# Attention blocks of the first tile: transposes, values and placing one round later, normalization last in its round

## Chip, core and metric

The kernel runs on one core of a Trainium2 chip. The time is device microseconds of one execution; the median of several runs is compared. A core has TensorE (PE, with its weight loads as PEld), VectorE (DVE), ScalarE (ACT), GpSimd (POOL) and SyncE (SP), which here only issues DMAs. Each engine takes its instructions in a fixed order and waits on semaphores of the others.

## What is computed

A chunked attention over 4 batches of 8 heads, 768 positions of 64 features, then two dense layers on the 3072 rows of 512 features:

```python
for c in range(nc):                      # chunks of 32 queries, context of 16 left and 8 right
    k_full = concatenate([mem_k, k_ctx]); v_full = concatenate([mem_v, v_ctx])   # 8 memory rows
    scores = scale * q_c @ k_full.T
    a = exp(scores - max(scores)); a = a / (sum(a) + 1e-9)
    out[c] = a @ v_full
x = out.transpose(0, 2, 1, 3).reshape(3072, 512)
h = x @ w_in;  x = (max(h, 0) + log1p(exp(-abs(h)))) @ w_out          # d_ff 2048
y = ((x @ w_a) * (x @ w_b)) @ w_o2                                    # d_ff 1536
```

q, k, v and the first weights come in as 64-bit floats.

## The kernel before

The 3072 rows are eight tiles of 384. For each tile the first layer runs over 16 slots `f`: `emit_h` (L465) makes `ph` with 12 matmuls, ACT and DVE form the softplus `g` in `emit_soft` (L471 to L475, L452, L455), and `emit_x1` (L488) accumulates. The second layer (L520, L540) follows for all eight tiles. Each operand is split in a high and a low part, so three matmuls stand for one product.

Weights arrive as 64-bit words in `raw`. `convert_a` (L102 on ACT, L104 and L105 on DVE) puts them together as 32-bit `tmp`, and `convert_b` (L112 on ACT, L113 on DVE) splits `tmp` into the parts of `w`. The buffers of `raw`, `w`, `work`, `qk` and `afb` are all of one pool of 33.

The attention of the first tile stands ahead of everything. It is cut in six blocks of 64 queries (`Block`), each with these steps:
- `turn`: PE transposes k and q (L278), ACT copies k (L281), DVE copies q (L283).
- `scores`: PE (L290), then DVE's masked row maxima, four of them (L325), then ACT's four exponentials with their sums (L329).
- `normal`: DVE, L333, L334 and L336.
- `flip`: PE transposes the normalized weights (L301), ACT copies them out (L302).
- `values`: PE, L309.
- `place`: ACT's cast (L315) and DVE's difference (L316) write the block's columns of the tile `x` that `emit_h` reads.

`ROUND` says in which order a round runs the steps and for which block: an entry (d, step) in round i is the step of block i - d. One `convert_a` goes behind `turn`, from round 1 on, and one `convert_b` behind `flip`, from round 2 on. What the rounds have not converted by then comes behind them, up to ten first halves and nine second halves. All five engines follow this order as it is written, up to the end of the first tile; the loads of the blocks and weights are issued by SP ahead of it, at most eight outstanding. The first tile's loop then mixes the 16 slots with conversions and with the attention steps of the second tile.

Of the kernel before, what the change touches and what calls it, by code (L numbers as in the profile page):

```python
# [25 lines left out]
               (1, "values"), (2, "place"))  # L26
EARLY, EARLY_AT, EARLY_BY = 3, 14.5, 8.25

ROUND = ((2, "normal"), (4, "place"), (0, "turn"), (2, "flip"), (1, "scores"), (3, "values"))
EARLY_RAW = (0, 1, 2, 3, 5, 7)  # L30
W_BY = (3, 2, 2, 2)
AHEAD = 6
# [7 lines left out]
def attn_moe_moe2(ctx: ExitStack, tc: tile.TileContext, q, k, v, mem_k, mem_v,  # L40
# [15 lines left out]
    BPT = TT // QB  # L56
# [492 lines left out]
    def order():  # L549
# [20 lines left out]
        def convert_1(half):  # L570
            if n_cv[half] < len(uses):
                (convert_a, convert_b)[half](*uses[n_cv[half]])
                n_cv[half] += 1

        for i in range(BPT + 4):
            for d, step in ROUND:
                if 0 <= i - d < BPT:
                    getattr(blocks[i - d], step)()
                if i >= CV_ROUND and step == "turn":
                    convert_1(0)  # L580
                if i > CV_ROUND and step == "flip":
                    convert_1(1)
# [79 lines left out]
        for fn, p in jobs:  # L662
            fn(*p)

    order()


# [28 lines left out]
```

## Time and profile before

| what | value |
|---|---|
| median of three runs | 1312.18 us (1309.62 to 1312.55) |
| profiled execution | 1311.32 us, span 1309.5 us |
| PE busy, share of the span | 1237.2 us, 94% |
| DVE, ACT, POOL busy | 473.4, 534.7, 247.6 us |
| chain that ended last, by engine | PE 84%, DVE 5%, SP's queue 3%, ACT 3%, DMA 3% |

The rows further down are from one profiled execution. Times are microseconds from the start of the span; 1.8 us of the profiled time lie outside the span. A busy time is an engine's own time in instructions; what an engine waits for is told in brackets behind the row. The ends of PE's rows are modelled.

### The profile page before, as it was taken

The page shows a single profiled execution, that of the slowest core. Times are in us where ns is not written, and L with a number is a line of the kernel's source. Part 1 is how long each engine was busy: PE and PEld are TensorE (multiplying, and loading weights), DVE is VectorE, ACT ScalarE, POOL GpSimd, SP SyncE. Part 2 cuts the span into 40 slices and gives each one's busy share as a digit, 9 for nine tenths or more (in the row PEclk, how much of TensorE's full clock was granted, in tenths as well). Part 3 has the DMA queues.
Part 4 walks back from the last instruction along what each step waited for, and adds up shares of the span by engine and source line. Part 5 has one row for each costly group of instructions (what it writes and reads, how often), then busy time and mean ns, then how long its engine had stood idle before and what let it go on. Part 6 is the DMA issues. An engine that isn't in the chain of part 4 may idle for free.

```text
span 1309.5 us, 20027 instructions
## 1 busy us (share of the span) xinstructions
PE 1237.2 (94%) x7872; PEld 1170.1 (89%) x7872; DVE 473.4 (36%) x1283; ACT 534.7 (41%) x1328; POOL 247.6 (19%) x233
## 2 busy tenths in 40 slices
PE   5768799999999999999798999999999999999998
PEld 4667699999999999999798999999999999999997
DVE  4767544544444454544678410111101011011100
ACT  4767556555556556554685211111111111111111
POOL 1000023223222322323001011211212121121111
PEclk9879899999999999999899999999999999999999
DMA  8872412213041312211775000010101001000000
GB/s 175 205 246 60 90 37 46 54 35 72 12 73 37 60 48 36 62 23 41 241 227 175 1 26 25 1 49 1 49 1 41 9 10 40 1 25 1 25 1 25
DMA packets 170169, 77.99 MB, mean 60 GB/s; under 512 B 137691, under 2 KB 162395, under 8 KB 170075
## 3 DMA queue, kind: packets, MB, share of 16 engines
q1 hardware_dynamic: 169563, 76.64, 22.1%
q8 instruction: 62, 1.02, 0.3%
q14 instruction: 32, 0.26, 0.1%
q0 software_dynamic: 512, 0.07, 0.0%
HBM read 64.09 MB, written 12.58 MB: 59 GB/s over the span
## 4 chain that ended last, share of the span: by engine, by line
PE 84%; DVE 5%; SPq 3%; ACT 3%; DMA 3%; issue 1%; DVEq 0%; ACTq 0%
PE pab L520 31%; PE ph L465 18%; PE px L488 17%; PE py L540 15%; DMA raw<-in_moe_w_out_dram 2%; PE sc L372 1%; PE pxa L415 1%; SPq L267 1%; DVE w L113 1%; DVE tmp L105 1%; ACT e L472 1%; SPq L264 1%; ACT e L471 1%; ACT e L473 1%; DVE g L475 0%
## 5 line engine op out<-in xcount | busy, mean ns | idle before, releaser
L520 PE MATMUL pab<-x,w 128*128 128x384 f32 x2304 | 418.8, 336 | 4.1 <-issue 4.1
L520 PEld LDWEIGHTS pab<-x,w 128*128 128x128 f32 x2304 | 405.9, 188 | 12.6 <-issue 4.4
L465 PE MATMUL ph<-x,w 128*128 128x384 f32 x1536 | 298.3, 342 | 13.5 <-ACT x L422 8.2
L465 PEld LDWEIGHTS ph<-x,w 128*128 128x128 f32 x1536 | 272.9, 192 | 20.1 <-ACT x L422 9.4
L529 DVE TENSOR_TENSOR c<-pab,a 128x384 f32<-128x384 f32 x96 | 53.6, 558 | 493.5 <-PE pab L520 493.5
L475 DVE SCALAR_TENSOR_TENSOR g<-ph,e 128x384 f32<-128x384 f32 x128 | 71.2, 557 | 257.0 <-ACT e L473 253.3
L527 ACT COPY a<-pab 128x384 f32<-128x384 f32 x96 | 46.1, 480 | 260.4 <-PE pab L520 260.4
L471 ACT ACTIVATE e<-ph 128x384 f32<-128x384 f32 x128 | 62.3, 486 | 132.2 <-PE ph L465 119.5
L390 DVE STREAM_TRANSPOSE af<-sm 32x256 f32<-32x256 f32 x180 | 78.2, 435 | 2.5
L473 ACT ACTIVATE e<-e 128x384 f32<-128x384 f32 x128 | 67.3, 526 | 3.8
L472 ACT ACTIVATE e<-e 128x384 f32<-128x384 f32 x128 | 67.3, 526 | 3.8
L329 ACT ACTIVATE sm<-sm,st 128x96 f32<-128x96 f32 x168 | 60.5, 362 | 4.7 <-DVE st L325 4.7
L505 POOL TENSOR_TENSOR x<-xr,x 128x1536 fp32r<-128x1536 f32 x8 | 28.4, 3554 | 153.5 <-DVE x L504 148.7
L105 DVE SCALAR_TENSOR_TENSOR tmp<-raw,tmp 128x512 uint32<-128x512 uint32 x68 | 50.2, 739 | 14.4 <-ACT raw L102 11.0
L113 DVE TENSOR_TENSOR w<-tmp,w 128x512 fp32r<-128x512 f32 x68 | 46.9, 689 | 16.9 <-ACT w L112 16.8
L102 ACT ACTIVATE raw<-raw 128x512 f32<-128x512 f32 x68 | 45.4, 673 | 15.4 <-DMA raw<-in_moe_w_in_dram 7.1
L112 ACT CAST w<-tmp 128x512 fp32r<-128x512 f32 x68 | 41.6, 613 | 17.2 <-DVE tmp L105 17.1
L195 POOL DMA_DIRECT2D mem_n<-in_mem_k_dram x16 | 8.9, 560 | 155.8 <-DVE mem_t L353 155.8
L336 POOL TENSOR_TENSOR sm<-sm,st 128x768 f32<-128x768 f32 x18 | 26.5, 1472 | 60.1 <-DVE st L334 46.9
L104 DVE TENSOR_SCALAR tmp<-raw 128x512 uint32<-128x512 uint32 x68 | 31.9, 469 | 5.0 <-DMA raw<-in_moe_w_in_dram 4.6
L325 DVE CUSTOM_DVE_ANT_0 sm<-sc,mask 128x96 f32<-128x96 f32 x168 | 31.4, 253 | 3.8 <-PE sc L372 3.8
L329 ACT ACTIVATION_READ_ACCUMULATOR sm<-sm,st 128x1 f32 x168 | 31.4, 187 | 0.0
(251 smaller groups left out, 1851.7 us busy)
## 6 DMA issues: line engine op xcount, KB each, us to landing
raw<-in_moe_w_out_dram SPq DMA_DIRECT2D x28, 512.0 KB
raw<-in_moe_w_in_dram SPq DMA_DIRECT2D x16, 512.0 KB
vn<-in_v_dram SPq DMA_DIRECT2D x35, 176.0 KB
raw<-in_moe_w_a_dram SPq DMA_DIRECT2D x12, 512.0 KB
x_scratch<-xo SPq DMA_DIRECT2D x32, 192.0 KB
xr<-x_scratch SPq DMA_DIRECT2D x8, 768.0 KB
raw<-in_moe_w_b_dram SPq DMA_DIRECT2D x12, 512.0 KB
out_dram<-yo SPq DMA_DIRECT2D x24, 256.0 KB
```

Source lines behind the costliest of these rows:

```text
L105: nc.vector.scalar_tensor_tensor(val, high, 3, val, ALU.logical_shift_left, ALU.bitwise_or)
L113: nc.vector.tensor_tensor(w[:, 1], val, w[:, 0].bitcast(F32), ALU.subtract)
L329: nc.scalar.activation(sm[:, h], sm[:, h], AF.Exp, bias=st[:, 0, h:h + 1], scale=-1.0, accum_out=st[:, 1, h:h + 1])
L390: nc.vector.transpose(out=af[32 * kb:32 * kb + 32, x], in_=self.sm[32 * x:32 * x + 32, :, 32 * kb:32 * kb + 32])
L465: nc.tensor.matmul(ph, lhsT=a, rhs=c, start=n == 0, stop=n == 3 * KT - 1)
L471: nc.scalar.activation(e, ph, AF.Abs)
L472: nc.scalar.activation(e, e, AF.Exp, scale=-1.0)
L473: nc.scalar.activation(e, e, AF.Ln, bias=1.0)
L475: nc.vector.scalar_tensor_tensor(g, ph, 0.0, e, ALU.max, ALU.add)
L488: nc.tensor.matmul(acc[t][i][:, :TT], lhsT=a, rhs=c, start=f == 0 and m == 0, stop=f == NF1 - 1 and m == 2)
L520: nc.tensor.matmul(p, lhsT=a, rhs=c, start=n == 0, stop=n == 3 * KT - 1)
L540: nc.tensor.matmul(acc[t][i], lhsT=a, rhs=c, start=f == 0 and m == 0, stop=f == NF2 - 1 and m == 2)
```

## The change

```diff
-ROUND = ((2, "normal"), (4, "place"), (0, "turn"), (2, "flip"), (1, "scores"), (3, "values"))
+ROUND = ((3, "flip"), (5, "place"), (0, "turn"), (1, "scores"), (2, "normal"), (4, "values"))
@@ in order()
-        for i in range(BPT + 4):
+        for i in range(BPT + 5):
             for d, step in ROUND:
                 if 0 <= i - d < BPT:
                     getattr(blocks[i - d], step)()
                 if i >= CV_ROUND and step == "turn":
                     convert_1(0)
                 if i > CV_ROUND and step == "flip":
                     convert_1(1)
```

A block's `flip`, `values` and `place` come one round later than before; `normal` stays in its round, but stands behind `scores` instead of ahead of all; `flip`, and with it `convert_b`, moves to the head of the round. There are eleven rounds instead of ten. From the first slot of the first tile's loop on, the order on each engine is the old one.

On ACT, rounds 4 to 6. Before, the round from the exponentials of block 3 (`work_339`) on: place, copy of k, first half of a conversion, copy of the transposes, cast:

```order
L329 ACTIVATE work_339<-work_339 128x96 x4
L315 CAST x_395<-pxb_442 128x4x64
L281 COPY work_456<-pt_5_457 128x384
L102 ACTIVATE raw_172<-raw_172 128x512
L302 COPY afb_473<-pat_474 96x512
L112 CAST w_480<-tmp_411 128x512
L329 ACTIVATE work_398<-work_398 128x96 x4
```

Now, from the same exponentials of block 3 on:

```order
L329 ACTIVATE work_339<-work_339 128x96 x4
L302 COPY afb_432<-pat_433 96x512
L112 CAST w_439<-tmp_399 128x512
L315 CAST x_442<-pxb_423 128x4x64
L281 COPY work_445<-pt_5_446 128x384
L102 ACTIVATE raw_172<-raw_172 128x512
L329 ACTIVATE work_386<-work_386 128x96 x4
```

The copy of the transposes and the cast moved from the end of the round to its head; the copy is now of block 2, not 3.

On DVE, the same place. Before, from the last read-out of block 3's maxima to the first maxima of block 4 (`work_398`):

```order
L325 ISA work_339 128x1
L333 TENSOR_SCALAR work_339<-work_339 128x4
L334 RECIPROCAL work_339<-work_339 128x4
L336 TENSOR_TENSOR work_339<-work_339 128x384
L316 TENSOR_TENSOR x_395<-pxb_442,x_395 128x4x64
L283 COPY qk_174<-pt_5_463 128x256
L104 TENSOR_SCALAR tmp_469<-raw_172 128x512
L105 SCALAR_TENSOR_TENSOR tmp_469<-raw_172,tmp_469 128x512
L113 TENSOR_TENSOR w_480<-tmp_411,w_480 128x512
L325 ISA work_398<-scb_483,mask_72 128x96
```

Now, from the last read-out of block 3's maxima to the first maxima of block 4 (`work_386`):

```order
L325 ISA work_339 128x1
L333 TENSOR_SCALAR work_292<-work_292 128x4
L334 RECIPROCAL work_292<-work_292 128x4
L336 TENSOR_TENSOR work_292<-work_292 128x384
L113 TENSOR_TENSOR w_439<-tmp_399,w_439 128x512
L316 TENSOR_TENSOR x_442<-pxb_423,x_442 128x4x64
L283 COPY qk_174<-pt_5_452 128x256
L104 TENSOR_SCALAR tmp_458<-raw_172 128x512
L105 SCALAR_TENSOR_TENSOR tmp_458<-raw_172,tmp_458 128x512
L325 ISA work_386<-scb_462,mask_72 128x96
```

The normalization behind block 3's maxima is that of block 2, and L113 moved from behind L105 to ahead of L316.

On DVE again, the end of the rounds, up to `g` of slot 0. Before, from the last place on:

```order
L316 TENSOR_TENSOR x_395<-pxb_591,x_395 128x4x64
L104 TENSOR_SCALAR tmp_602<-raw_202 128x512
L105 SCALAR_TENSOR_TENSOR tmp_602<-raw_202,tmp_602 128x512
L113 TENSOR_TENSOR w_606<-tmp_584,w_606 128x512
L104 TENSOR_SCALAR tmp_609<-raw_204 128x512
L105 SCALAR_TENSOR_TENSOR tmp_609<-raw_204,tmp_609 128x512
L113 TENSOR_TENSOR w_613<-tmp_602,w_613 128x512
L104 TENSOR_SCALAR tmp_631<-raw_214 128x512
L105 SCALAR_TENSOR_TENSOR tmp_631<-raw_214,tmp_631 128x512
L475 SCALAR_TENSOR_TENSOR g_0_639<-ph_0_616,e_0_635 128x384
```

Now, from the place before the last on:

```order
L316 TENSOR_TENSOR x_442<-pxb_580,x_442 128x4x64
L104 TENSOR_SCALAR tmp_594<-raw_202 128x512
L105 SCALAR_TENSOR_TENSOR tmp_594<-raw_202,tmp_594 128x512
L113 TENSOR_TENSOR w_607<-tmp_594,w_607 128x512
L316 TENSOR_TENSOR x_442<-pxb_598,x_442 128x4x64
L104 TENSOR_SCALAR tmp_612<-raw_204 128x512
L105 SCALAR_TENSOR_TENSOR tmp_612<-raw_204,tmp_612 128x512
L104 TENSOR_SCALAR tmp_631<-raw_214 128x512
L105 SCALAR_TENSOR_TENSOR tmp_631<-raw_214,tmp_631 128x512
L475 SCALAR_TENSOR_TENSOR g_0_639<-ph_0_616,e_0_635 128x384
```

The last place stands behind the second half of the weight whose first half is just ahead of it (`tmp_594`), where it stood ahead of both before.

## Rows read from the trace of the kernel before

**Rows 1.** Busy time by stage: stretch, length, each engine's busy us, clock, DMA share, GB/s.

```profile
0.00:53.00 53.00, 30.38 (x265) 23.32 (x265) 29.57 (x138) 27.75 (x85) 3.91 (x15) 0.96 0.85 189
...
161.00:1309.50 1148.50, 1124.66 (x7032) 1068.87 (x7032) 370.08 (x968) 434.73 (x1067) 240.01 (x212) 0.99 0.17 46
```

**Rows 2.** Timeline of round 3: start, duration, engine, line, operation, [idle before, releaser].

```profile
25.35 0.68 ACT L102 ACTIVATE raw<-raw 128x512 f32<-128x512 f32 x1 [2.57 <-DMA raw<-in_moe_w_in_dram]
...
26.06 0.69 DVE L105 SCALAR_TENSOR_TENSOR tmp<-raw,tmp 128x512 uint32<-128x512 uint32 x1 [0.28 <-ACT raw L102]
...
27.65 0.25 DVE L325 CUSTOM_DVE_ANT_0 work<-scb,mask 128x96 f32<-128x96 f32 x1
```

**Rows 3.** Timeline of round 5, from block 3's maxima to block 4's.

```profile
33.48 0.25 DVE L325 CUSTOM_DVE_ANT_0 work<-scb,mask 128x96 f32<-128x96 f32 x1
...
34.16 1.52 PE L278 MATMUL pt<-ident,qk 96*128 96x96 f32 x8
34.19 0.09 DVE L325 DVE_READ_ACCUMULATOR2_ANT work<- 128x1 f32 x1
...
35.35 0.17 DVE L333 TENSOR_SCALAR work<-work 128x4 f32<-128x4 f32 x1 [1.07 <-ACT work L329]
...
35.76 0.56 DVE L336 TENSOR_TENSOR work<-work 128x384 f32<-128x384 f32 x1
...
36.24 0.42 DVE L316 TENSOR_TENSOR x<-pxb,x 128x256 fp32r<-128x256 f32 x1
...
36.47 1.06 PE L301 MATMUL pat<-ident,work 128*96 128x128 f32 x4 [0.80 <-DVE work L336]
36.57 0.41 DVE L283 COPY qk<-pt 128x256 f32<-128x256 f32 x1
...
37.43 0.69 DVE L105 SCALAR_TENSOR_TENSOR tmp<-raw,tmp 128x512 uint32<-128x512 uint32 x1
...
37.46 1.55 PE L290 MATMUL scb<-work,qk 64*64 64x96 f32 x16
37.57 0.58 ACT L302 COPY afb<-pat 96x512 f32<-96x512 f32 x1 [1.06 <-PE pat L301]
38.05 0.62 ACT L112 CAST w<-tmp 128x512 fp32r<-128x512 f32 x1
...
38.70 0.69 DVE L113 TENSOR_TENSOR w<-tmp,w 128x512 fp32r<-128x512 f32 x1 [0.58 <-ACT w L112]
...
39.31 0.25 DVE L325 CUSTOM_DVE_ANT_0 work<-scb,mask 128x96 f32<-128x96 f32 x1
```

**Rows 4.** Timeline from the last place to the first `g` of the loop.

```profile
52.58 0.42 DVE L316 TENSOR_TENSOR x<-pxb,x 128x256 fp32r<-128x256 f32 x1
...
53.05 5.57 PE L465 MATMUL ph<-x,w 128*128 128x384 f32 x23 [0.82 <-DVE x L316]
...
56.57 0.49 ACT L471 ACTIVATE e<-ph 128x384 f32<-128x384 f32 x1 [1.20 <-PE ph L465]
...
58.21 0.56 DVE L475 SCALAR_TENSOR_TENSOR g<-ph,e 128x384 f32<-128x384 f32 x1 [0.37 <-ACT e L473]
```

**Rows 5.** Timeline: the last block's transposes on PE.

```profile
48.12 0.61 PE L301 MATMUL pat<-ident,work 128*96 128x128 f32 x4 [2.27 <-DVE work L336]
```

**Rows 6.** Chain to 62 us: start, length, what; weights from issue to landing.

```profile
56.39 6.12 DMA raw<-in_moe_w_out_dram
```

**Rows 7.** Timeline of ACT: the first half of the conversion of these weights.

```profile
63.52 0.68 ACT L102 ACTIVATE raw<-raw 128x512 f32<-128x512 f32 x1
```

**Rows 8.** Waits from 53 to 160 us: who for whom, total us, times, longest.

```profile
ACT raw L102 <- DMA raw<-in_moe_w_a_dram: 6.1, 1, 6.1
```

**Rows 9.** Waits of SP's queue in the same stretch.

```profile
SPq L185 <- DVE kt L358: 17.0, 1, 17.0
```

**Rows 10.** Chain from 86 to 98 us.

```profile
89.97 3.75 PE ph L465 x12
...
95.80 2.10 PE ph L465 x12
```

## The prediction

> **What bounds the kernel now.** I read the busy time by stage first [rows 1]. From 161 us to the end TensorE is busy 1124.66 of 1148.50 us, so nothing that ends before can be made good there: a microsecond won or lost before 161 us is one at the end, unless a wait in between swallows it. The change sits in the first 53 us, where no engine is full: PE 30.38, DVE 29.57, ACT 27.75 us of 53, the DMA engines at 0.85. So this stage is a chain that goes from engine to engine, and the timeline is the view to take it from.
>
> In the first three rounds the loads set the pace: in round 3 the raw weights land at 25.35, ACT's L102 and DVE's L105 follow, and then DVE waits for the cast of the previous weights, so that its row maxima (L325) start at 27.65 [rows 2]. From round 4 on the loads are ahead and a round takes 39.31 - 33.48 = 5.83 us [rows 3]. In it DVE waits twice: 1.07 us before L333, for ACT's four exponentials, and 0.58 us before L113, for ACT's cast L112, which stands behind the copy L302 and with it behind PE's transpose L301. The change moves both.
>
> **Round with the new order.** The old round is: maxima, exponentials (ACT), normalization, place, L283, L104, L105, cast, L113, maxima. The new one (order rows of DVE and ACT in the section on the change) begins with the transposes of the block that was normalized at the very end of the round before, and ACT does the copy of that transpose and the cast L112 next. DVE's first instruction of the round, L113, needs that cast. So the 1.07 us wait goes, and a longer one takes its place: L113 stands behind PE and two ACT instructions that start only when the normalization ends. Counting starts to starts in [rows 3], with N the end of L336:
> - N to PE's transpose 36.47 - 36.32 = 0.15; the transpose 1.06; to ACT's copy 0.04; copy to cast 38.05 - 37.57 = 0.48; cast 0.62; to L113 0.03. Together L113 starts at N + 2.38, with DVE idle all the while (its next instructions are queued behind L113).
> - L113 to its successor 39.31 - 38.70 = 0.61; L316 to L283 0.33; L283 over L104 to L105 0.86; L105 to the maxima 0.61 (I take L113's figure, both last 0.69). The maxima start at N + 4.79.
> - Maxima to L333: the last read-out starts at 34.19, so 0.71; L333 to the start of L336 35.76 - 35.35 = 0.41; L336 0.56: 1.68.
>
> A new round takes 6.47 us with all parts, 6.14 without L316 (rounds 3 and 4) and 6.14 without L283 (from round 6), against 5.83. The transposes and scores on PE and the copies and exponentials on ACT fit beside it: PE ends the scores at about N + 4.2 (0.15, then 0.99 from transpose to the next group, 1.52 for the turn, 1.55 for the scores), before N + 4.79, and the exponentials that are used have a whole round. That is the cover I count on, by little: 0.6 us.
>
> **Where the rounds land.** In round 3 the landing at 25.35 is the same. L105 starts at 26.06, and now the maxima follow it at once, 26.67 instead of 27.65: a lead of 0.98 us. Then the rounds cost it back. Maxima of round 4: 26.67 + 6.14 = 32.81 (33.48 before); round 5: + 6.47 = 39.28 (39.31 before): a draw. Round 6: + 6.47 - 0.33 = 45.42, against 39.31 + 5.83 = 45.14 at the old pace.
>
> **The tail.** This is the term that decides. Before, the maxima of the last block were followed by its exponentials and normalization at once, its values came one round later and its place two, and the last place (L316) started at 52.58 [rows 4]. Now block 5 is normalized in round 7, transposed in round 8, multiplied in round 9 and placed in round 10:
> - Round 6: N = 45.42 + 1.68 = 47.10. Round 7: L113 at 49.48, L316 50.09, L105 50.95 (without L283, L104 takes its place behind L316), normalization from 51.56 to 52.53. Round 8: L113 at 54.91, L316 55.52, L105 56.38.
> - Rounds 9 and 10 are conversions and places alone, in the order second half, place, first half. The second half of one weight now waits for the first half of the same one: L105 0.69 + 0.03, cast 0.62 + 0.03, L113 0.61, L316 to L105 0.86 = 2.84 us each. Before, the next first half stood between them and hid it. Round 9 has L105 at 59.22; in round 10 L113 is at 60.59 and the last L316 at 61.20.
>
> That is 8.6 us after 52.58. Some of that is conversions that used to come behind the last L316 and now come before it. What counts is g, the first product of ACT's chain on ph. Before, PE's 12 matmuls got going at 53.05, ACT's L471 started 3.52 us later at 56.57, and DVE's L475 at 58.21; DVE was nearly there by itself, since it waited 0.37 us only [rows 4]. Now the matmuls go at 61.20 + 0.47 = 61.67, L471 at 65.19 if PE is as slow as it was, and L475 at 66.83: **8.6 us later**. DVE alone would be ready at 61.20 + 0.86 (to L105 of raw9) + 0.61 + 0.53 (L104 and L105 of raw10) + 0.61 = 63.81, 5.6 us later than before. So the shift lies between 5.6 and 8.6, by PE's speed in ph; I take 8.6.
>
> **Clock.** In round 5 a transpose group of four took 1.06 us, and at 48.12 one of the same shape took 0.61 [rows 3, 5]. I read the first as the lower level (1.2 GHz) and the second as the higher (2.4 GHz). The change leaves PE with less work per us, so I keep 1.06. The Trainium skill, "TensorE: Matmul & The Clock Gate", section "What's actually happening", has it that the throttled clock is the default and that activity releases it; by that the thinner rounds would stay at 1.06 and the sum stands, while a released clock would give 0.45 us back for every transpose on the chain.
>
> **What carries the shift on.** From 58 us on the first tile's loop runs in the same order on every engine. A load that lands just in time would swallow a gain, not a loss: the weights issued at 56.39 land at 62.51 and are taken at 63.52, 1.0 us later [rows 6, 7]. Further on ACT waits 6.1 us for the first w_a weights [rows 8]. That could swallow a shift, but the queue that loads them is itself released by DVE's L358, for which it waited 17.0 us [rows 9]; so that wait moves along. The buffers that the loads take are other ones now; their users are done by the time the queue, which goes at the pace of the loads, gets there. I cost this at nothing; the price if one is late is that the queue stands for about a round, under loads that are wanted 5 us later and more.
>
> So: profiled execution 1311.3 + 8.6 = 1319.9. It lies 0.9 us under the median of the runs shown (1312.18, from 1309.62 to 1312.55); I forecast 1320.0.
>
> **Rivals.**
> - *PE faster than assumed.* Two transposes of the tail at 0.61 instead of 1.06 (-0.9) and ph at the higher clock (2.10 us for its 12 matmuls, as at 95.80 [rows 10], instead of 3.52: -1.4; DVE allows up to -3.0): 1317.6. For it: the 0.61 row [rows 5]. Against: PE is idler than before from 47 to 61 us, and ph ran slowly behind such a stretch before.
> - *The alignment of slow clock stretches with later work.* A group of ph took 3.75 us at 89.97 and 2.10 at 95.80 [rows 10]; the wait patterns of the first tile's loop move against the clock's changes. One such group more or fewer is +1.7 or -1.7: 1318.3 to 1321.7. It goes with either case.
> - *Swallowed.* If the w_a loads were issued at a time of their own, ACT's 6.1 us would take the shift down to 2.5: 1313.8, no measurable change. Against it stands the 17.0 us wait of the queue.
> - *Faster.* If the cast came early, because ACT and PE ran beside the normalization instead of behind it, a round would be DVE's own work, 5.83 - 1.07 - 0.58 = 4.18 us, and the tail would be reached some 4 us earlier. It decides from the point where the transpose no longer waits for the L336 just ahead of it. The order speaks against it: the block that is transposed is the one normalized last. And the loads would allow about 1 us of it [rows 6, 7]: 1310.3; over 2.6 us would need luck with the clock on top.
> - *It does nothing.* The order shows that it moves every round.
>
> **How the numbers follow.** A measurement of this kernel can tell about 0.2%, 2.6 us, from no change. Forecast (shift 8.6, alignment within 1.7) 0.62; PE faster 0.23; swallowed 0.08; faster or level for the reason above 0.05; the remaining 0.02 is a late buffer that costs more. From the first two, nearly all slower by over 2.6 us, and the 0.02: slower 0.86. Swallowed and most of the last rival are within: 0.11. Faster 0.03. The low end of the range is the smallest shift, 5.6, less 1.7: 1315.2. The high end is 8.6, plus 1.7, plus about 1 if ph of the second slot is slow too, plus the 0.9 by which the median stands above the profiled execution: 1323.5.
>
> **What would show it.** Right: DVE's L113 idle ahead by about 2.3 us in rounds 4 to 8, ended by ACT's L112; no wait left before L333; maxima at about 32.8, 39.3 and 45.4; the last L316 near 61; the first L475 of the loop near 66.8; the same distance from L475 to the end of the span. Wrong: rounds under 5.8 us, a last L316 before 57, or a w_a wait on ACT that has shrunk from 6.1 us by as much as the start got later.

## The result and the profile after

| what | before | after |
|---|---|---|
| median of the runs | 1312.35 us (1309.62 to 1314.34, 5 runs) | 1319.73 us (1317.58 to 1321.62, 5 runs) |
| profiled execution | 1311.32 us, span 1309.5 | 1320.95 us, span 1319.1 |
| first `g` of the loop (L475) | 58.21 | 65.01 |

The ratio is 1.0057, with an interval from 1.0038 to 1.0076: the changed kernel is slower by 7.4 us, against a forecast of 1320.0 us, 7.8 us over the median shown ahead of it.

The busy times by stage of the changed kernel (stretch, length, busy us of PE, PEld, DVE, ACT, POOL, then clock, DMA share, GB/s) answer to [rows 1]:

```profile
0.00:53.00 53.00, 28.03 (x248) 22.51 (x248) 26.63 (x132) 25.48 (x80) 3.91 (x15) 0.76 0.87 199
170.00:1319.10 1149.10, 1125.55 (x7031) 1069.82 (x7030) 369.44 (x967) 435.00 (x1067) 239.79 (x210) 0.99 0.17 46
```

In the first 53 us every engine of the attention has done less than before (DVE 26.63 against 29.57 us). The granted clock shown is 0.76 against 0.96; that PE ran more slowly in the rounds does not follow from it, as the point on the clock further down says. In the stretch behind it (set to start 9 us later than that of [rows 1], as the stage ends later) PE is as full as it was: 23.6 us of it idle, against 23.8. So what was lost early stayed lost.

The timeline of a full round after the change, from block 3's maxima to block 4's (start, duration, engine, line, operation, idle before and releaser), answers to [rows 3]:

```profile
30.64 0.25 DVE L325 CUSTOM_DVE_ANT_0 work<-scb,mask 128x96 f32<-128x96 f32 x1
...
31.35 0.17 DVE L333 TENSOR_SCALAR work<-work 128x4 f32<-128x4 f32 x1
31.76 0.56 DVE L336 TENSOR_TENSOR work<-work 128x384 f32<-128x384 f32 x1
...
32.47 1.06 PE L301 MATMUL pat<-ident,work 128*96 128x128 f32 x4 [1.60 <-ACT work L329]
33.56 0.58 ACT L302 COPY afb<-pat 96x512 f32<-96x512 f32 x1 [1.09 <-PE pat L301]
34.04 0.62 ACT L112 CAST w<-tmp 128x512 fp32r<-128x512 f32 x1
34.69 0.69 DVE L113 TENSOR_TENSOR w<-tmp,w 128x512 fp32r<-128x512 f32 x1 [2.37 <-ACT w L112]
...
37.10 0.25 DVE L325 CUSTOM_DVE_ANT_0 work<-scb,mask 128x96 f32<-128x96 f32 x1
```

L333 follows the maxima without a wait: the 1.07 us of [rows 3] are gone. In their place DVE stands 2.37 us ahead of L113, and the rows between show for what: the transpose L301, the copy L302 and the cast L112, one after the other, from the end of the normalization on. The round takes 37.10 - 30.64 = 6.46 us, against 5.83.

The end of the attention after the change, from block 5's maxima on, from the same timeline, answers to [rows 4]:

```profile
43.22 0.25 DVE L325 CUSTOM_DVE_ANT_0 work<-scb,mask 128x96 f32<-128x96 f32 x1
...
55.53 0.69 DVE L113 TENSOR_TENSOR w<-tmp,w 128x512 fp32r<-128x512 f32 x1 [0.68 <-ACT w L112]
...
58.98 0.42 DVE L316 TENSOR_TENSOR x<-pxb,x 128x256 fp32r<-128x256 f32 x1
...
63.38 0.49 ACT L471 ACTIVATE e<-ph 128x384 f32<-128x384 f32 x1 [3.64 <-PE ph L465]
...
65.01 0.56 DVE L475 SCALAR_TENSOR_TENSOR g<-ph,e 128x384 f32<-128x384 f32 x1 [3.35 <-ACT e L473]
```

The last place is 58.98 - 52.58 = 6.4 us later than in [rows 4], and `g` 6.8 us. The two tail rounds take 2.84 us each, with DVE idle 0.68 us in each for the cast of the weight whose first half it has just made.

### The profile page after: what moved, and what is told of

Same layout as the page of the kernel before. It is cut to its first block, busy times and chain, and to the rows that moved or that the text cites. A ratio compares the mean times of both kernels' runs of the same rounds, so it can differ in the third digit from the quotient of the medians.

```text
span 1319.1 us, 20034 instructions
## 1 busy us (share of the span) xinstructions
PE 1240.9 (94%) x7872; PEld 1174.8 (89%) x7872; DVE 472.9 (36%) x1283; ACT 535.4 (41%) x1328; POOL 248.0 (19%) x233
## 4 chain that ended last, share of the span: by engine, by line
PE 84%; DVE 5%; SPq 3%; ACT 3%; DMA 2%; issue 1%; DVEq 0%; ACTq 0%
PE pab L520 31%; PE ph L465 18%; PE px L488 17%; PE py L540 15%; PE sc L372 1%; DVE tmp L105 1%; DVE w L113 1%; PE pxa L415 1%; SPq L267 1%; DMA raw<-in_moe_w_in_dram 1%; ACT e L472 1%; SPq L264 1%; ACT e L471 1%; DVE g L475 1%; ACT e L473 1%
## 5 line engine op out<-in xcount | busy, mean ns | idle before, releaser
L475 DVE SCALAR_TENSOR_TENSOR g<-ph,e 128x384 f32<-128x384 f32 x128 | 71.3, 557 | 261.8 <-ACT e L473 258.1
L471 ACT ACTIVATE e<-ph 128x384 f32<-128x384 f32 x128 | 62.3, 487 | 135.8 <-PE ph L465 123.8
L329 ACT ACTIVATE sm<-sm,st 128x96 f32<-128x96 f32 x168 | 60.5, 361 | 4.7 <-DVE st L325 4.7
L113 DVE TENSOR_TENSOR w<-tmp,w 128x512 fp32r<-128x512 f32 x68 | 46.9, 689 | 31.3 <-ACT w L112 31.3
L105 DVE SCALAR_TENSOR_TENSOR tmp<-raw,tmp 128x512 uint32<-128x512 uint32 x68 | 50.2, 739 | 14.3 <-ACT raw L102 10.7
L112 ACT CAST w<-tmp 128x512 fp32r<-128x512 f32 x68 | 41.5, 613 | 19.1 <-DVE tmp L105 19.0
L336 POOL TENSOR_TENSOR sm<-sm,st 128x768 f32<-128x768 f32 x18 | 26.5, 1472 | 60.1 <-DVE st L334 46.9
```

Source lines behind the costliest of these rows:

```text
L105: nc.vector.scalar_tensor_tensor(val, high, 3, val, ALU.logical_shift_left, ALU.bitwise_or)
L113: nc.vector.tensor_tensor(w[:, 1], val, w[:, 0].bitcast(F32), ALU.subtract)
L329: nc.scalar.activation(sm[:, h], sm[:, h], AF.Exp, bias=st[:, 0, h:h + 1], scale=-1.0, accum_out=st[:, 1, h:h + 1])
L471: nc.scalar.activation(e, ph, AF.Abs)
L475: nc.vector.scalar_tensor_tensor(g, ph, 0.0, e, ALU.max, ALU.add)
```

## The experiments

Each kernel was timed against the kernel before, which had medians from 1311.1 to 1311.4 us beside them. In what follows a kernel's tail is the time from block 5's maxima to the last L316.

### A later round alone

```diff
-ROUND = ((2, "normal"), (4, "place"), (0, "turn"), (2, "flip"), (1, "scores"), (3, "values"))
+ROUND = ((2, "normal"), (5, "place"), (0, "turn"), (3, "flip"), (1, "scores"), (4, "values"))
-        for i in range(BPT + 4):
+        for i in range(BPT + 5):
```

> One part of the change alone: transposes, values and place one round later and eleven rounds, but the old order within a round (normalization first, transposes behind the first half of the conversion). My theory (the cost comes from the normalization at the end of a round with the transposes of the same block right behind it, which puts the cast L112 and with it L113 behind PE): the 1.07 us wait before L333 stays, the wait before L113 goes, a full round takes 5.83 - 0.58 = 5.2 us, the last place L316 starts near 51.5 (52.58 before), and the time is 1 us below the kernel before, 1311, not to be told from it. Rival (an extra round is what costs, whatever its order): one more round of 5.8 us, last L316 near 58, 1318.

Measured: 1309.82 us, ratio 0.9992 (0.9983 to 1.0000). DVE's timeline of this kernel, a full round from block 3's maxima on, block 5's maxima, and the end:

```profile
30.10 0.25 DVE L325 CUSTOM_DVE_ANT_0 work<-scb,mask 128x96 f32<-128x96 f32 x1
...
31.97 0.17 DVE L333 TENSOR_SCALAR work<-work 128x4 f32<-128x4 f32 x1 [1.08 <-ACT work L329]
...
34.66 0.68 DVE L113 TENSOR_TENSOR w<-tmp,w 128x512 fp32r<-128x512 f32 x1
35.26 0.25 DVE L325 CUSTOM_DVE_ANT_0 work<-scb,mask 128x96 f32<-128x96 f32 x1
...
40.09 0.25 DVE L325 CUSTOM_DVE_ANT_0 work<-scb,mask 128x96 f32<-128x96 f32 x1
...
49.05 0.42 DVE L316 TENSOR_TENSOR x<-pxb,x 128x256 fp32r<-128x256 f32 x1
...
55.08 0.56 DVE L475 SCALAR_TENSOR_TENSOR g<-ph,e 128x384 f32<-128x384 f32 x1 [1.97 <-ACT e L473]
```

The wait before L333 stays, L113 waits for nothing, and the full round takes 5.16 us, as expected (the next one, without L283, 4.83). The last L316 is 2.5 us earlier than the 51.5 on record, which had been counted from a profile with a late start (second profile, below). The eleventh round alone is no loss.

### The new order without the later round

```diff
-ROUND = ((2, "normal"), (4, "place"), (0, "turn"), (2, "flip"), (1, "scores"), (3, "values"))
+ROUND = ((2, "flip"), (4, "place"), (0, "turn"), (1, "scores"), (1, "normal"), (3, "values"))
```

> The other part alone, as far as it can stand alone: ten rounds and the old distances for transposes, values and place, but transposes and cast at the head of the round and the normalization as its last work on DVE (it has to be one round earlier then, behind the maxima of its own block). My theory: DVE waits 1.07 us for the exponentials and then 2.38 us for the cast, a full round takes 6.47 + 1.1 = 7.6 us, the last L316 starts between 58 and 60.5, and the time is 5 to 8 us above the kernel before, 1317 to 1320. Rival (the extra round costs): ten rounds, no cost, 1312.

Measured: 1323.22 us, ratio 1.0090 (1.0077 to 1.0103). DVE's timeline, one round and the end:

```profile
35.56 0.25 DVE L325 CUSTOM_DVE_ANT_0 work<-scb,mask 128x96 f32<-128x96 f32 x1
...
37.42 0.17 DVE L333 TENSOR_SCALAR work<-work 128x4 f32<-128x4 f32 x1 [1.07 <-ACT work L329]
...
40.77 0.69 DVE L113 TENSOR_TENSOR w<-tmp,w 128x512 fp32r<-128x512 f32 x1 [2.37 <-ACT w L112]
...
43.18 0.25 DVE L325 CUSTOM_DVE_ANT_0 work<-scb,mask 128x96 f32<-128x96 f32 x1
...
61.97 0.42 DVE L316 TENSOR_TENSOR x<-pxb,x 128x256 fp32r<-128x256 f32 x1
...
68.00 0.56 DVE L475 SCALAR_TENSOR_TENSOR g<-ph,e 128x384 f32<-128x384 f32 x1 [1.49 <-ACT e L473]
```

Both waits stand in one round of 7.62 us, as expected; the last L316 and the whole came out later than on record (61.97 against 58 to 60.5, and +12 against +5 to +8 us). The order is the part that costs. This kernel is not just the rest of the change, though: it normalizes a block a round earlier than the change does, and so pays for both waits. In the full change the normalization is that of a block whose exponentials were done a round ago, which takes the 1.07 us out of the round, and a round is 6.46.

### The cast ahead of the transposes

The changed kernel, with the second half of a conversion issued ahead of the flip instead of behind it:

```diff
             for d, step in ROUND:
                 if 0 <= i - d < BPT:
+                    if i > CV_ROUND and step == "flip":
+                        convert_1(1)
                     getattr(blocks[i - d], step)()
+                elif i > CV_ROUND and step == "flip":
+                    convert_1(1)
                 if i >= CV_ROUND and step == "turn":
                     convert_1(0)
-                if i > CV_ROUND and step == "flip":
-                    convert_1(1)
```

> The changed kernel with one suspected wait taken off: the second half of the conversion is issued ahead of the transposes of its round, so the cast L112 no longer stands behind the copy L302; all else as changed. My theory: the wait before L113 goes from 2.38 to about 0.3 us, the next one in the chain (L316 behind ACT's place cast, or L283 behind PE's turn) then stops DVE at about N + 2.0 to 2.7; full rounds take 5.5 to 5.9 us instead of 6.46, the last L316 starts some 3 us earlier than in the changed kernel (58.98), near 56, and the time is 3 us below the changed kernel, 1316 to 1317. Rival (extra round): unchanged, 1319.7.

Measured: 1315.98 us, ratio 1.0033 (1.0022 to 1.0045). DVE's timeline, one round and the end:

```profile
37.78 0.69 DVE L113 TENSOR_TENSOR w<-tmp,w 128x512 fp32r<-128x512 f32 x1 [0.70 <-ACT w L112]
39.14 0.42 DVE L316 TENSOR_TENSOR x<-pxb,x 128x256 fp32r<-128x256 f32 x1 [0.67 <-ACT x L315]
...
54.68 0.42 DVE L316 TENSOR_TENSOR x<-pxb,x 128x256 fp32r<-128x256 f32 x1
```

The wait before L113 falls from 2.37 to 0.70 us (0.3 was expected), and 0.67 us of it comes back one instruction further on, since ACT's copy and cast L315 still stand behind the transposes. More than a third of the loss is gone (4.7 us over the kernel before are left of 7.4): that L113 waited for PE at all came from ACT's order.

### The flip back in the middle of the round

The changed kernel, with one entry moved:

```diff
-ROUND = ((3, "flip"), (5, "place"), (0, "turn"), (1, "scores"), (2, "normal"), (4, "values"))
+ROUND = ((5, "place"), (0, "turn"), (3, "flip"), (1, "scores"), (2, "normal"), (4, "values"))
```

> The changed kernel with its flip (and the second halves of the conversions that follow it) behind the turn, where the kernel before has it, instead of at the head of the round; everything else of the change stays, the normalization last too. Theory (the cost is that the head of the round waits for the normalization just ahead of it): no wait of VectorE before L113 over 0.3 us and none before L333 from round 4 on, rounds of 4.2 to 5.1 us (VectorE's own work in a round is 5.83 - 1.07 - 0.58 = 4.18 us; TensorE's, by what the rows of the rounds show at its lower level, is 5.1), last L316 at 49 to 50.5 against 58.98. Since the loads are then what is late, little of it reaches the end: 1309 to 1311 us, ratio 0.998 to 1.000. Rival (to normalize a round later than the exponentials and to place two rounds later is what costs, wherever the flip stands): the last L316 stays near 55 to 57, and 1316 to 1318 us.

Measured: 1310.89 us, ratio 0.9995 (0.9986 to 1.0003). DVE's timeline, one round and the end:

```profile
35.34 0.69 DVE L113 TENSOR_TENSOR w<-tmp,w 128x512 fp32r<-128x512 f32 x1 [0.53 <-ACT w L112]
...
36.65 0.17 DVE L333 TENSOR_SCALAR work<-work 128x4 f32<-128x4 f32 x1
...
38.07 0.42 DVE L316 TENSOR_TENSOR x<-pxb,x 128x256 fp32r<-128x256 f32 x1 [0.44 <-ACT x L315]
...
40.55 0.25 DVE L325 CUSTOM_DVE_ANT_0 work<-scb,mask 128x96 f32<-128x96 f32 x1
...
51.23 0.42 DVE L316 TENSOR_TENSOR x<-pxb,x 128x256 fp32r<-128x256 f32 x1
...
57.12 0.56 DVE L475 SCALAR_TENSOR_TENSOR g<-ph,e 128x384 f32<-128x384 f32 x1 [2.49 <-ACT e L473]
```

With the normalization last and eleven rounds, but the flip behind the turn, the whole loss is gone: about 8 us between this kernel and the changed one (-0.5 and +7.4 us, each by its own median of the kernel before), for the place of one step and of the casts that follow it. From block 2's maxima to block 5's its rounds take 5.24, 5.15 and 4.60 us, the last without L283; the waits on DVE before L113 are a little longer than expected (up to 0.53 us, and 0.91 in the round behind the last maxima), and the last L316 is 0.7 us past the range on record.

### First halves first in the tail

The changed kernel, from round 9 on:

```diff
-                if i >= CV_ROUND and step == "turn":
+                if i >= CV_ROUND and step == ("turn" if i < BPT + 3 else "flip"):
                     convert_1(0)
-                if i > CV_ROUND and step == "flip":
+                if i > CV_ROUND and step == ("flip" if i < BPT + 3 else "turn"):
                     convert_1(1)
```

> The changed kernel, but from round 9 on the first half of a conversion comes ahead of the second half, so that the two places that are left no longer wait for the halves of one weight in a row. Theory: the 0.68 us waits of VectorE before L113 in rounds 9 and 10 go or shrink to under 0.2, the last L316 is at 58.0 instead of 58.98, g of slot 0 by as much earlier, and the time 1 us less, 1318.7 us; that part of the change is then a tenth of the whole. Rival (the halves' order in the tail is the main cost): 1314 us or less.

Measured: 1319.84 us, ratio 1.0059 (1.0047 to 1.0072). The 0.68 us waits are gone from the trace, and the tail is 58.39 - 43.53 = 14.86 us against 58.98 - 43.22 = 15.76, 0.9 less as expected. This execution was 0.3 us behind by block 5's maxima, so that the last L316 is only 0.6 us earlier. In the median nothing of it is to be seen. The time of so small a part stays inconclusive; that it is not the main cause is clear.

### TensorE kept busy up to `ph`

The changed kernel with spare transposes behind the values, 30 in the first run (10, 6, 14) and 59 in the second:

```diff
+        def spare(i, n):
+            p = ps.tile([P, 512], F32, tag="acc0", name=f"spare{i}", bufs=1)
+            for k in range(n):
+                nc.tensor.transpose(p[:, :P], ident, ident)
...
+                if step == "values" and BPT + 1 <= i <= BPT + 3:
+                    spare(i, (13, 12, 34)[i - BPT - 1])
```

> The changed kernel with 30 more transposes of the identity on PE, 10, 6 and 14 behind the values of rounds 7, 8 and 9, where PE is idle; they write a PSUM bank that nobody reads. It puts a price on PE's slow start: in the changed kernel the 12 matmuls of the first ph are granted 1.2 GHz and ACT's L471 starts 4.40 us behind the last L316. My theory: with PE busy ahead of it ph runs at 2.4 GHz, L471 comes 1.6 to 2.3 us earlier, the first L475 of the loop near 63, and the time falls by about 2 us, to 1317.5. Rival (L475 is held by DVE or ACT, not by PE): L475 stays 6 us behind the last L316 and the time stays at 1319.7.

> The changed kernel with 59 spare transposes on TensorE (13, 12 and 34 behind the values of rounds 7, 8 and 9), so that it works nearly up to the first matmuls of ph; 30 of them ended 3.3 us too early for that. What it prices is the lower clock level in ph. Theory (ph is slow because TensorE stood idle ahead of it): the group of 12 of slot 0 takes 2.1 to 2.4 us, ScalarE's L471 starts 2.6 to 3.1 us behind the last L316 instead of 4.40, VectorE is the next thing late, g of slot 0 at 62.8 to 63.6 instead of 65.01, and the time 1317 to 1318.5 us. Rival (the level does not follow what TensorE did just before): L471 stays 4.0 us or more behind, and the time within 1 us of the changed kernel's.

Measured: 1318.33 us, ratio 1.0059 (1.0045 to 1.0072), with 30, and 1317.27 us, ratio 1.0047 (1.0034 to 1.0059), with 59. The timeline with 30 spare transposes, behind the last of them:

```profile
58.15 0.44 PE L465 MATMUL ph<-x,w 128*128 128x384 f32 x1 [2.53 <-ACT x L315]
...
62.49 0.49 ACT L471 ACTIVATE e<-ph 128x384 f32<-128x384 f32 x1 [3.25 <-PE ph L465]
```

and with 59:

```profile
47.15 3.04 PE L578 MATMUL spare<-ident 128*128 128x128 f32 x13
...
51.68 1.53 PE L578 MATMUL spare<-ident 128*128 128x128 f32 x12
...
54.00 3.93 PE L578 MATMUL spare<-ident 128*128 128x128 f32 x34
...
59.06 4.28 PE L465 MATMUL ph<-x,w 128*128 128x384 f32 x23 [0.35 <-DVE x L316]
...
61.30 0.49 ACT L471 ACTIVATE e<-ph 128x384 f32<-128x384 f32 x1 [1.94 <-PE ph L465]
62.94 0.56 DVE L475 SCALAR_TENSOR_TENSOR g<-ph,e 128x384 f32<-128x384 f32 x1 [1.67 <-ACT e L473]
```

With 30, PE stood 2.53 us before `ph`, the granted clock was 0.50 from 60 to 62 us, and L471 came 62.49 - 58.47 = 4.02 us behind the last L316: nearly nothing was won there, a miss. With 59 the granted clock was 1.00, 23 of the first 24 matmuls took 4.28 us (the pace of the 12 in 2.10 us of [rows 10]), L471 came 61.30 - 58.60 = 2.70 us behind the last L316 instead of 4.40, and `g` at 62.94, as expected; but VectorE was not the next thing late, since L475 still waited 1.67 us for ACT. So PE's lower clock level in `ph` is worth 1.7 us here. It is no part of the loss: `ph` was as slow in the kernel before (6.04 us from the last L316 to `g` in its second profile, below, against 6.03 in the changed kernel). With the 59 spares, which also shortened block 5's transposes from 1.06 to 0.62 us, the changed kernel is still 5.9 us above the kernel before (1317.27 against 1311.36 us).

### A second profile of both kernels

No edit in either.

> The kernel before, unchanged, profiled a second time. Its profile had the raw weights of round 3 at 25.33 us, and every other kernel of this study had them at 22.6 to 23.0. Theory (the landing differs from execution to execution): 22.6 to 23.0 here, round 3 about 1 us or more earlier, and the last L316 at 50 to 52 instead of 52.58. Rival (the landing belongs to the order of the kernel before): 25.3 again. The time is 1309.6 to 1314.4 us either way.

> The changed kernel, unchanged, profiled a second time. Its waits before L113 should be 2.37 us again in every full round and the tail rounds 2.84 us, since they are worked out from durations. What may differ is when the first rounds run (up to 2 us) and where the stretches at the lower clock lie behind 89 us: if these move, g of slot 0 keeps its distance to the last L316 (6.0 us) but the distance from there to the end of the span differs by 1 to 2 us from 1254.1; if they don't, it is 1254.1 within 0.5.

The second execution of the kernel before took 1314.19 us (span 1312.4), that of the changed one 1319.71 us (span 1317.9). Timeline of the kernel before, second profile, round 3, block 5's maxima and the end:

```profile
22.84 0.68 ACT L102 ACTIVATE raw<-raw 128x512 f32<-128x512 f32 x1 [0.43 <-DMA raw<-in_moe_w_in_dram]
...
43.08 0.25 DVE L325 CUSTOM_DVE_ANT_0 work<-scb,mask 128x96 f32<-128x96 f32 x1
...
50.97 0.42 DVE L316 TENSOR_TENSOR x<-pxb,x 128x256 fp32r<-128x256 f32 x1
...
57.01 0.56 DVE L475 SCALAR_TENSOR_TENSOR g<-ph,e 128x384 f32<-128x384 f32 x1 [0.77 <-ACT e L473]
```

The load of round 3 that [rows 2] show at 25.35, after 2.57 us of waiting, was there at 22.84: it differs by execution, not by order. The last L316 of the kernel before is then at 50.97, as expected. The changed kernel's second profile has its last L316 at 58.34 and `g` at 64.37, again 6.03 us apart, with 2.37 us waits (1.93 in one round) and tail rounds of 2.84 us; from its last L316 to the end of the span it is 1259.6 us, against 1260.1 in the first profile. (The 1254.1 expected is the distance from `g` to the end; that is 1253.5 here.) So two profiles of the changed kernel agree within 0.6 us there, and two profiles of the kernel before do not, from `g` to the end: 1251.3 and 1255.4 us. Where these 4.1 us lie is told at the end.

### The two gains together

The kernel before with the later round alone and 56 spare transposes (24, 6 and 26):

```diff
+ROUND = ((2, "normal"), (5, "place"), (0, "turn"), (3, "flip"), (1, "scores"), (4, "values"))
...
+                if step == "values" and BPT + 1 <= i <= BPT + 3:
+                    spare(i, (24, 6, 26)[i - BPT - 1])
```

> The kernel before with transposes, values and placing one round later (as in the run that moved nothing else) and with 56 spare transposes on TensorE (24, 6 and 26 behind the values of rounds 7, 8 and 9), so that it works up to the matmuls of ph. It puts together the two things that made g of slot 0 earlier so far. Theory (the first stage can still give time): the last L316 at 49.0 as there, L471 1.7 us closer to it, at 51.7 to 52.5 instead of 53.44, g at 53.5 to 54.2 instead of 55.08; if all of that reaches the end, 1308.5 us against 1309.8 without the spares and about 1311.3 for the kernel before, ratio 0.997 to 0.9985. Rival (the loads are what is late by then, since weights were awaited until 51.70 in that run): g at 54.3 or later, and the time as without the spares, 1309.8 within 0.5.

Measured: 1311.21 us, ratio 0.9998 (0.9988 to 1.0007). Timeline at the end of the attention:

```profile
52.08 0.68 ACT L102 ACTIVATE raw<-raw 128x512 f32<-128x512 f32 x1 [2.71 <-DMA raw<-in_moe_w_in_dram]
...
54.27 0.56 DVE L475 SCALAR_TENSOR_TENSOR g<-ph,e 128x384 f32<-128x384 f32 x1 [0.79 <-ACT e L473]
```

`g` is at 54.27, 2.7 us earlier than in the kernel before's second profile and 3.9 earlier than in [rows 4], and the time is the same. Neither side had it right: `g` lies between the two, and the time is 1.4 us above the rival's 1309.8. The loads do bound `g` by now, since ACT stood 2.71 us for weights that are queued ahead of L471. What took the rest of the lead behind `g` is not shown: from `g` to the end this execution took 1255.9 us, where two executions of the kernel before took 1251.3 and 1255.4. No version of this study beats the kernel before by more than a measurement tells.

## Why the prediction was right

It was right in its sign, its size and its mechanism. The start of the rounds was off by 1.7 us and the alignment of slow stretches by about 1 us; that they made up for each other in the profiled execution, which ended within 1.1 us of the 1319.9 added up for it, is luck. What is not luck is the shift of 7.4 us between the medians: against the second profile of the kernel before, `g` came 7.4 and 8.0 us later in the two profiles of the changed one. Point by point:

- **L113 at N + 2.38.** Measured 2.37 to 2.38 us of idle time ahead of it in five of the six rounds with a flip, 1.93 in one (next point). No wait before L333 is left. Right.
- **The length of a round.** Predicted 6.14 without L316, 6.47 in full, 6.14 without L283. Measured, from the maxima at 18.83, 24.96, 30.64, 37.10 and 43.22: 6.13, 5.68, 6.46, 6.12. The 5.68 is a round in which one flip ran at the higher clock level (0.62 us at 26.78). Right, with that one exception.
- **Where the rounds start: wrong by 1.7 us.** The step that failed is "in round 3 the landing at 25.35 is the same". In the changed kernel's execution the weights were taken at 23.12 without a wait, and the maxima of round 3 stood at 24.96, not 26.67. The second profile of the kernel before shows that its own landing had been late by chance. So the maxima, the last L316 and `g`, which were to be seen near 32.8, 39.3, 45.4, 61 and 66.8, all came 1.8 to 2.2 us earlier than that. A sum of differences should have been made against a round that no load sets.
- **A draw by block 5's maxima.** Predicted 45.42 against 45.14 (45.13 in the trace). Measured, in executions whose loads were on time, 43.22 and 42.58 against 43.08. Right: up to there the change neither costs nor gains.
- **The tail decides.** Predicted 61.20 - 45.42 = 15.78 us; measured 58.98 - 43.22 = 15.76. In the kernel before it is 52.58 - 45.13 = 7.45 in the first profile and 50.97 - 43.08 = 7.89 in the second. So the tail grows by 7.9 to 8.3 us, against 8.34 on record, and that is the whole loss. The experiments say of what: 8.96 us with the later round alone (from 40.09 to 49.05), 10.68 with all of the change but the flip in the middle (from 40.55 to 51.23), 15.76 with the flip at the head. In the first two the quicker rounds had made up for the longer tail before it began (block 5's maxima at 40.09 and 40.55). Block 5's maxima in the first profile of the kernel before:

```profile
45.13 0.25 DVE L325 CUSTOM_DVE_ANT_0 work<-scb,mask 128x96 f32<-128x96 f32 x1
```

- **`ph` behind the last place.** Predicted 5.63 us from L316 to `g`, as in [rows 4]; measured 6.03 in both profiles of the changed kernel, and 57.01 - 50.97 = 6.04 in the second profile of the kernel before. PE was slow in `ph`, as taken, and by 0.4 us more than in [rows 4]; what [rows 4] show was the fast end for a slow `ph`.
- **The sum.** Against the second profile: 43.22 - 43.08 + 7.87 + 0 = 8.0 us. Against the first: 43.22 - 45.13 + 8.31 + 0.40 = 6.8 us. On record: 0.28 + 8.34 + 0 = 8.6.
- **The clock.** The chain ran at the lower level (1.2 GHz), as taken: transposes of 1.06 to 1.09 us in five of the six rounds with a flip. That is not the work of thinner rounds, since in the kernel before five of six took 1.06 us as well, one of them in [rows 3], with a granted clock of 0.96 over the stretch [rows 1]. Until its first fall, at 49 us in the kernel before and at 28 us in the changed one, the clock is shown as 1.00 whatever the matmuls take. So 0.96 and 0.76 do not tell at which level the rounds ran; the times of matmuls of one shape do. What the Trainium skill has in "TensorE: Matmul & The Clock Gate", section "What's actually happening", is that the throttled clock is the default and that activity releases it. The run with 59 spare transposes agrees: its first 13 took 3.04 us, and with PE at work nearly all the time the next 12 took 1.53 us. The rival "PE faster" gets its price from the 59 spare transposes: 1.7 us at L471 where 1.4 was on record; it did not come about by itself.
- **What carries the shift on.** Right in its mechanism: ACT's wait for the first w_a weights is still 6.0 us, since the queue that loads them again waits for DVE's L358, which came at 138.06 instead of 130.16; the queue's next load was issued 7.9 us later with it (138.48 and 130.59). The waits of the changed kernel from 53 to 168 us (who for whom, total, times, longest) answer to [rows 8] and [rows 9]:

```profile
ACT raw L102 <- DMA raw<-in_moe_w_a_dram: 6.0, 1, 6.0
...
SPq L185 <- DVE kt L358: 18.6, 1, 18.6
```

- **Losses passed, a gain of 2.7 us did not.** It stood there as "would swallow a gain, not a loss". Set against the second profile of the kernel before, `g` moved by +11.0, +7.4 to +8.0, +3.6 us (the order alone, the change, the cast first), and the medians by +12.0, +7.4, +4.7; with 30 and 59 spares it is +7.1 and +5.9 in both. In the other direction `g` moved by -1.9 and -2.7 us (the later round alone, and with spare transposes), and the medians by -1.4 and +0.1, each known to about 1 us. So one gain reached the end in the main and the other did not. A load that swallows a gain behind `g` is not shown by any of these runs.
- **The alignment of slow stretches.** Put at 1.7 us either way. The profiled execution of the changed kernel is 9.6 us longer than that of the kernel before, 2.8 more than its first `g` is later, and the kernel before differs from itself by 4.1 us. Mis-sized by 1 us and more. A median over several executions is less at its mercy than a pair of profiles.

## What to carry to other kernels

A step moved to the head of a round starts no earlier if what it needs was just moved to the end of the round before: count starts to starts around the loop, and count for every in-order queue what stands behind the moved step. Here the same eleven rounds cost nothing with the transposes in the middle and about 8 us more with them at the head. And price the tail by itself: rounds can end in a draw while the last blocks, which nothing follows, pay for every round added.

## What the runs showed of the hardware

Two executions of one and the same program can differ by several us. The chain of work in the kernel before (start, length, what), first profile:

```profile
119.17 1.05 PE pa L404 x8
120.22 2.11 PE px L488 x12
```

and second profile:

```profile
118.23 1.91 PE pa L404 x8
120.14 3.82 PE px L488 x12
```

The same 20 instructions took 3.16 us once and 5.73 us the other time. The granted clock from 118 to 122 us was 1.00 in the first and 0.50 in the second. Ahead of them PE had stood 2.50 us for DVE's L336 in the first and 3.87 us in the second. These 2.6 us are most of the 4.1 us by which the two executions differ from the first `g` to the end. In the same way the raw weights of round 3 were there at 25.35 in one execution of the kernel before and at 22.84 in the other. A sum made against one profiled execution holds such chances in its base; a second profile of the same kernel shows which terms they are.
